# Loading the values of later batches with a casting DMA in GpSimd's queue, in one file with q, k and the expert weights

## Chip, cores and metric

The kernel runs on one NeuronCore of a Trainium2 chip. The metric is device time in microseconds (us), the median of several executions. Smaller is better.

## Reference

Sparse attention in four batches is followed by a mixture of experts that sends a whole batch (a "sentence") to one expert. Cut to what matters:

```python
# q, k, v: (4, 8, 768, 64) fp32
k_sum = k.reshape(B, H, 24, 32, D).max(axis=3)      # one key per block of 32
v_sum = v.reshape(B, H, 24, 32, D).mean(axis=3)     # one value per block
scores_l = q @ k.T / 8, kept where |i - j| < 16     # window
scores_s = q @ k_sum.T / 8 + log(32)                # all 24 blocks
x = softmax([scores_l, scores_s]) @ [v, v_sum]      # (4, 768, 512) over the heads
# experts: w1 (8, 512, 1024), w2 (8, 1024, 512) fp32
logits = x.mean(axis=1) @ w_gate                    # one row per batch
e = argmax(logits); gate = softmax(logits)[e]
out = gate * (relu(x @ w1[e]) @ w2[e])
```

The weights of a batch can be fetched only when its own attention is complete, since the gate chooses the expert.

## The kernel before

**Attention.** A batch has 8 heads in 4 pairs and 768 queries in 12 groups (j) of 64. One group needs 96 window keys and 24 block keys, 120 rows. For a pair, TensorE transposes k (L406) and q (L431), VectorE copies k out of PSUM with the windows laid side by side (L425; ScalarE does that for batch 0, L423) and q (L439), and takes the block maxima (L445). Per pair and half (6 groups) TensorE makes scores (L463), ScalarE the exponential (L474), VectorE multiplies by the mask (L478), TensorE multiplies by the values (L496, called AV here) and VectorE normalizes (L509, L510). Each pair is then transposed (L520) and copied to `xT_b` (L528).

**Values.** The operand of AV is `vblk`, 128 partitions x 12 groups x 8 heads x 65 in bf16, two buffers by the parity of the batch. Rows 16 to 79 of a group are its own 64 values, rows 0 to 15 and 80 to 95 the neighbours' (the halo), rows 96 to 119 the 24 block sums, and column 64 is one, for the softmax's denominator. For batches 1 to 3, SyncE's queue loads v in fp32 into the single buffer `v_f`, one DMA per head (L211). VectorE casts two heads at a time into `vblk` (L295), SyncE copies the halo inside `vblk` (L300, L301), TensorE sums the blocks with the matrix `bind` (L355), VectorE casts the sums to `vsb` (L367), and two DMAs spread them to all 12 groups (L374). Batch 0 loads its halo from HBM.

**Experts.** After the gate (L633 to L694) GpSimd reads the chosen expert's number (L653) and issues the loads of w1 (L664) and w2 (L670), cast to bf16 by the DMA. TensorE makes the hidden layer (L725, 16 half tiles a batch, ScalarE's relu at L740) and the output (L759, 6 tiles, called o; ScalarE scales them at L769 and SyncE stores them, L772). q and k come through GpSimd's queue too, cast by the DMA (L204).

**Order.** The program adds operations with durations and dependencies to a list scheduler, `Sched`. At build time it gives each engine a fixed order. Every engine then runs its own list in order: an instruction that waits holds up all that stand behind it on its engine. `after` fixes only the order of two issues. The file of GpSimd's DMAs is: the chosen w1 and w2 of batch b, the second half of q and k of b+1, the first half of b+2. The loads of v for b+2 stand in SyncE's queue, behind the issue of w2 of b.

Of the kernel before, what the change touches and what calls it, by code (L numbers as in the profile page):

```python
# [12 lines left out]
BF16 = mybir.dt.bfloat16  # L13
# [8 lines left out]
class Sched:  # L22


    SEM = 0.06
    URGENT = 3.0

    def __init__(self):
        self.ops = []
# [37 lines left out]
    def run(self, t0):  # L67
        free = dict(t0)
        rings = {}
        left, users = {}, {}  # L70
        for op in self.ops:
            need = {d["n"] for d in op["deps"] + op["after"]}
            left[op["n"]] = len(need)
            for n in need:
                users.setdefault(n, []).append(op)
        tail = {}
        for op in reversed(self.order(users)):
            tail[op["n"]] = op["dur"] + op["lat"] + (op["dma"] and op["dma"] + 2.0) + max(
                [tail[u["n"]] for u in users.get(op["n"], [])], default=0.0
            )  # L80
# [12 lines left out]
        for op in self.ops:  # L93
            if not left[op["n"]]:
                push(op)
        for _ in self.ops:
            best = None
            for eng, rs in ready.items():
                if not rs:
                    continue  # L100
                t0e = max(free.get(eng, 0.0), min(r for r, _ in rs))
                pick = None
                for r, op in sorted(rs, key=lambda x: x[1]["key"]):
                    start = max(t0e, r)
# [12 lines left out]
            free[eng] = t + op["dur"]  # L117
            op["issued"] = t + op["dur"]
            op["end"] = op["issued"] + op["lat"]
            if op["dma"]:  # L120
                begin = max(rings.get(eng, 0.0), op["issued"] + 0.8)
                other = max([f for e, f in rings.items() if e != eng], default=0.0)
                shared = min(op["dma"], max(0.0, other - begin))
                rings[eng] = begin + op["dma"] + shared
                op["end"] = rings[eng] + 1.2
# [9 lines left out]
def kernel(  # L135
# [10 lines left out]
    nc = tc.nc  # L146
# [5 lines left out]
    QB = 64  # L152
# [55 lines left out]

    def load_v(b, h):
        if b > 0:  # L210
            nc.sync.dma_start(v_f[16:80, :, h, :], v[b, h].rearrange("(j p) d -> p j d", p=QB))  # L211
            return
        j0 = 1 if h == 0 else 0
        nc.sync.dma_start(  # L214
            v_f[:, j0:NJ, h, :],
            bass.AP(
                tensor=v.tensor,
                offset=v.offset + (h * S + j0 * QB - 16) * D,
                ap=[[D, 80], [QB * D, NJ - j0], [1, D]],
            ),  # L220
        )
        if h == 0:
            nc.sync.dma_start(v_f[16:80, 0, 0, :], v[0, 0, 0:QB, :])
# [41 lines left out]
    def setup_dve():  # L265
        for i in range(2):
            nc.vector.memset(vblks[i][64:KW, NJ - 1, :, :], 0.0)
            nc.vector.memset(vblks[i][0:KW, :, :, D : D + 1], 1.0)
        for t in kts:
# [56 lines left out]
    def v_ops(b, loads):  # L326
# [4 lines left out]
        groups = [(0,), (1,)] if b == 0 else [(0, 1)]  # L331
        casts = []
        for c in range(NP):
            on_act = False
            eng = nc.scalar if on_act else nc.vector
            casts.append(
# [5 lines left out]
                )  # L342
            )
        for gs in groups:
            cs = [c for g in gs for c in casts[2 * g : 2 * g + 2]]
# [5 lines left out]
            def vs(b=b, gs=gs, st=st):  # L351
                ps = ops_pool.tile([128, 512], FP32, name="ops")
                for j in range(NJ):
                    for i, hg in enumerate(gs):
                        nc.tensor.matmul(  # L355
                            ps[32 * i : 32 * i + 32, 0 : HW * (D + 1)],
                            lhsT=bind[:, j, :],
                            rhs=vblks[b % 2][0:80, j, hg * HW : (hg + 1) * HW, :],
                            start=(j == 0),
                            stop=(j == NJ - 1),  # L360
                        )
                st["ps"] = ps

            def ev(b=b, gs=gs, st=st):
                n = 32 * len(gs)
                st["sb"] = sm_pool.tile([64, HW, D + 1], BF16, name="vsb")
                nc.vector.tensor_copy(  # L367
                    st["sb"][0:n],
                    st["ps"][0:n, 0 : HW * (D + 1)].rearrange("p (h c) -> p h c", c=D + 1),
                )  # L370

            def bc(b=b, gs=gs, st=st):
                for i, hg in enumerate(gs):
                    nc.sync.dma_start(  # L374
                        vblks[b % 2][KW:NR, :, hg * HW : (hg + 1) * HW, :],
                        st["sb"][32 * i : 32 * i + NB].unsqueeze(1).to_broadcast([NB, NJ, HW, D + 1]),
                    )
# [3 lines left out]
            o_ev = add("DVE", 0.42, [o_vs], ev)  # L381
            sl["first"], sl["readers"] = o_vs, [o_ev]
            o_bc = add("SP", 0.6 * len(gs), [o_ev], bc, dma=0.8 * len(gs))
            for g in gs:
                done.append([hl, o_bc])
        v_ready[b] = done
# [235 lines left out]

        return sequence, xsl, x_ops

    def gate(b, x_ops, w_deps):

        sb = state[b]
        sl, deps = sch.slot("ops", 1)
# [66 lines left out]

        o_lg = add("PE", 0.25, x_ops + deps, lgf, lat=0.2)
        o_mx = add("DVE", 0.7, [o_lg], mxf)
        o_ld = add("POOL", 1.5, [o_mx] + w_deps, ldf)
# [90 lines left out]
        return [o_st(st) for st in range(NST)]  # L789

    casts, bcs = v_ops(0, v_loads)
    moe_last = {}
    w_order = []
    for b in range(B):
        sch.prio = 40.0 if b == 0 else 0.0
        sequence, xsl, x_ops = attention(b)
        nxt = b + 1
        sch.prio = 0.0
        if nxt < B:
            prev = last_T.get(nxt - 2, [])  # L800
            qk_loads[nxt, 0] = qk_loads[nxt, 1] = add(
                "POOL", 1.3, prev, lambda n=nxt: load_qk(n, 0, 4), dma=4.7, after=order_pool
            )
            vl = []
            for h in range(H):
                vl.append(
                    add("SP", 0.6, casts, lambda n=nxt, h=h: load_v(n, h), dma=0.87, after=vl[-1:] + bcs + w_order)
                )

        sch.prio = 40.0 if b == 0 else 0.0  # L810
        sequence()
        w = gate(b, x_ops, moe_last.get(b - 2, []))
        w_order = [w[2]]
        sch.prio = 0.0
        if nxt < B:
            casts, bcs = v_ops(nxt, vl)
            qk_loads[nxt, 2] = qk_loads[nxt, 3] = add(
                "POOL", 1.3, prev, lambda n=nxt: load_qk(n, 4, 8), dma=4.7,
                after=[w[2], qk_loads[nxt, 0]],
            )  # L820
            order_pool = [qk_loads[nxt, 2]]
        moe_last[b] = moe(b, w, xsl)

    sch.run({"PE": 0.0})
# [30 lines left out]
```

## Time and profile before

| What | us |
|---|---|
| Three executions | 228.34, 229.96, 229.79 |
| Median | 229.79 |
| Profiled execution | 229.69 |
| Its span, first to last instruction | 228.1 |
| TensorE busy | 163.5 (72%) |
| VectorE, ScalarE busy | 100.9, 96.9 |
| Mean granted TensorE clock | 0.892 |

The page divides the span into 40 slices of 5.7 us and gives busy shares in tenths. A row of the waits gives who waited for whom, the total in us, how often, and the longest wait. A row of the timeline gives start, duration, engine, line, operation and operands, and in brackets the idle time just before it and what ended that. The row of a DMA queue gives packets, MB and the time its packets took as a share of 16 DMA engines' time in the window.

### The profile page before, as it was taken

Reading aid. Unit: us, or ns where it says so; the run is one execution under the profiler, and the core shown is the slowest. Engines: PE = TensorE matmul, PEld = TensorE weight load, DVE = VectorE, ACT = ScalarE, POOL = GpSimd, SP = SyncE. Lnnn points to the kernel's source line nnn. Section 1 sums busy time; section 2 is a strip of 40 time slices with the busy share of each in tenths; the row PEclk is TensorE's granted clock in tenths of the full one; section 3 lists DMA queues with packets and bytes.
Section 4 is the critical chain, followed back from the end, with each engine's and each line's share of the span. In section 5 each row is a group of like instructions: output and inputs, shape, how many; then the busy total and the mean of one; then the engine's idle time right before and its main releaser. Section 6 shows DMA issues by size and latency. Waiting matters only on the chain.

```text
span 228.1 us, 4604 instructions
## 1 busy us (share of the span) xinstructions
PE 163.5 (72%) x1938; PEld 97.3 (43%) x1960; DVE 100.9 (44%) x207; ACT 96.9 (42%) x182; POOL 24.6 (11%) x43
## 2 busy tenths in 40 slices
PE   0266797478770598993890588994998999089992
PEld 0244675354440465551450455542455544045540
DVE  5364788961302978740302969501269611000000
ACT  2121675334431265553140266623467954025532
POOL 7226000340000000240000000220000002000000
PEclk9999999999995559998598579999799999659998
DMA  6999994299999604399999703199970016990033
GB/s 105 206 183 166 213 174 84 32 165 171 207 197 192 80 3 73 89 156 222 200 196 179 204 0 67 50 166 237 252 139 3 3 50 151 251 194 3 0 152 124
DMA packets 46870, 30.45 MB, mean 133 GB/s; under 512 B 28225, under 2 KB 42145, under 8 KB 46753
## 3 DMA queue, kind: packets, MB, share of 16 engines
q0 software_dynamic: 13264, 14.68, 40.3%
q1 hardware_dynamic: 33584, 15.47, 32.2%
q8 instruction: 15, 0.25, 0.5%
q14 instruction: 7, 0.05, 0.1%
HBM read 36.06 MB, written 6.29 MB: 186 GB/s over the span
## 4 chain that ended last, share of the span: by engine, by line
PE 36%; DMA 28%; SPq 15%; DVE 10%; ACT 5%; issue 3%; POOL 1%; POOLq 1%; ACTq 0%; DVEq 0%
DMA v_f<-in_v_dram 15%; PE hps L725 11%; DMA q_nat<-in_q_dram 9%; SPq L211 9%; PE hps L759 8%; DMA w_sb<-in_moe_w_dram 5%; SPq L214 4%; PE ops L355 3%; PE tps L520 3%; PE tps L431 3%; DVE kT L425 3%; PE kps L406 3%; DVE vblk L295 2%; PE sc L463 2%; PE ops L496 2%
## 5 line engine op out<-in xcount | busy, mean ns | idle before, releaser
L725 PE MATMUL hps<-xT_b,w_sb 128*128 128x256 bf16 (+1 forms) x242 | 55.2, 371 | 14.3 <-DMA w_sb<-in_moe_w_dram 12.6
L740 ACT ACTIVATE hT_sb<-hps 128x512 bf16<-128x512 f32 (+1 forms) x64 | 29.8, 489 | 38.2 <-PE hps L725 36.8
L759 PE MATMUL hps<-w_sb,hT_sb 128*128 128x512 bf16 x184 | 43.2, 380 | 0.6 <-issue 0.3
L725 PEld LDWEIGHTS <-w_sb 128*128 128x128 bf16 x256 | 24.7, 108 | 30.3 <-DMA w_sb<-in_moe_w_dram 12.5
L474 ACT ACTIVATE aT<-sc 128x768 bf16<-128x768 f32 x32 | 25.9, 809 | 14.9 <-PE sc L463 14.6
L406 PE MATMUL kps<-identb,k_nat 96*64 96x96 bf16 x256 | 11.3, 249 | 25.5 <-DVE kT L425 18.0
L478 DVE TENSOR_TENSOR aT<-aT,mask 120x768 bf16<-120x768 bf16 x32 | 17.7, 556 | 23.0 <-ACT aT L474 22.9
L295 DVE CAST vblk<-v_f 80x1536 bf16<-80x1536 f32 x16 | 15.2, 956 | 26.4 <-DMA v_f<-in_v_dram 26.4
L759 PEld LDWEIGHTS <-hT_sb 128*128 128x128 bf16 x192 | 17.8, 98 | 19.8 <-issue 0.2
L769 ACT ACTIVATE o_sb<-hps,gcol 128x512 f32<-128x512 f32 x24 | 16.5, 686 | 22.4 <-PE hps L759 15.4
L528 ACT ACTIVATE xT_b<-tps 128x768 bf16<-128x768 bf16 x16 | 13.0, 810 | 27.4 <-PE tps L520 27.4
L406 PEld LDWEIGHTS <-k_nat 96*64 96x64 bf16 x256 | 9.4, 139 | 28.0 <-issue 20.6
L664 POOL DMA_DIRECT2D w_sb<-in_moe_w_dram x5 | 3.8, 757 | 156.9 <-DVE grec L684 116.8
L496 PE MATMUL ops<-vblk,aT 120*64 120x65 bf16 x384 | 14.4, 220 | 7.2 <-DMA vblk<-vsb 4.1
L510 DVE TENSOR_TENSOR xs<-ops,rv 128x384 bf16<-128x384 f32 x32 | 17.8, 557 | 1.1
L496 PEld LDWEIGHTS <-aT 120*64 120x64 bf16 x384 | 10.8, 130 | 16.4 <-DVE xs L510 4.7
L425 DVE COPY kT<-kps 128x1152 bf16<-128x1152 bf16 x12 | 16.1, 1346 | 0.5 <-PE kps L406 0.5
L463 PE MATMUL sc<-qT,kT 64*128 64x64 bf16 x384 | 13.8, 215 | 3.0 <-ACT aT L474 1.6
L445 DVE TENSOR_REDUCE kmx<-kT 128x24 bf16<-128x768 bf16 x16 | 15.1, 942 | 0.1
L355 PE MATMUL ops<-vblk,bind 80*32 80x260 bf16 x96 | 11.3, 348 | 5.1 <-DVE vblk L295 5.1
L463 PEld LDWEIGHTS <-kT 64*128 64x128 bf16 x384 | 9.7, 109 | 10.6 <-issue 7.1
L509 DVE RECIPROCAL rv<-ops 128x6 f32<-128x6 f32 x32 | 6.1, 191 | 15.7 <-PE ops L496 15.6
(53 smaller groups left out, 110.6 us busy)
## 6 DMA issues: line engine op xcount, KB each, us to landing
w_sb<-in_moe_w_dram POOLq DMA_DIRECT2D x7, 1024.0 KB, 14.8
out_dram<-o_sb SPq DMA_DIRECT2D x24, 256.0 KB, 2.0
v_f<-in_v_dram SPq DMA_DIRECT2D x24, 192.0 KB, 8.5
k_nat<-in_k_dram POOLq DMA_DIRECT2D x6, 384.0 KB, 19.4
q_nat<-in_q_dram POOLq DMA_DIRECT2D x6, 384.0 KB, 20.9
v_f<-in_v_dram SPq DMA_DIRECT2D x7, 240.0 KB, 6.7
vblk<-vsb SPq DMA_DIRECT2D x8, 146.2 KB
vblk<-vblk SPq DMA_DIRECT2D x6, 178.8 KB, 3.8
```

The costliest lines, as they stand in the source:

```text
L211: nc.sync.dma_start(v_f[16:80, :, h, :], v[b, h].rearrange("(j p) d -> p j d", p=QB))
L295: eng.tensor_copy(dst, v_f[:, :, hs, :])
L355: nc.tensor.matmul(ps[32 * i : 32 * i + 32, 0 : HW * (D + 1)], lhsT=bind[:, j, :], rhs=vblks[b % 2][0:80, j, hg * HW : (hg + 1) * HW, :], ...
L406: nc.tensor.transpose(kps[hh * D : (hh + 1) * D, g, 2 : 2 + SP], qk_nat[b][1][:, 2 * pr + hh, g, :], identb[0:SP, 0:SP],)
L425: nc.vector.tensor_copy(kdst, win)
L463: nc.tensor.matmul(sc[:, hh, jj * QB : (jj + 1) * QB], lhsT=sb["kT"][pr][rs, j, :], rhs=sb["qT"][pr][rs, j, :], start=True, stop=True, til ...
L474: nc.scalar.activation(aT, sb["sc"][:, :, 0 : NH * QB], ACT.Exp, scale=SCALE)
L496: nc.tensor.matmul(ops[(j % 2) * QB : (j % 2 + 1) * QB, hh, jj // 2, :], lhsT=aT[0:NR, hh, jj * QB : (jj + 1) * QB], rhs=vb[0:NR, j, 2 * p ...
L510: nc.vector.tensor_tensor(out=sb["xs"][pr][:, hf * NS : (hf + 1) * NS, :, :].rearrange("p s h d -> p h s d"), in0=ops[:, :, :, 0:D], in1=r ...
L725: nc.tensor.matmul(sb["hps"][:, 0 : c1 - c0], lhsT=sb["w1"][:, dt, ft * 128 : (ft + 1) * 128], rhs=sb["xT"][:, dt, c0:c1], start=(dt == 0) ...
L740: nc.scalar.activation(sb["hT"][:, ft, c0:c1], ps["t"][:, 0 : c1 - c0], ACT.Relu)
L759: nc.tensor.matmul(ps["t"], lhsT=sb["hT"][:, ft, st * 128 : (st + 1) * 128], rhs=sb["w2"][:, ft, :], start=(ft == 0), stop=(ft == NFT - 1),)
```

## The change

For batches 1 to 3, v is loaded by GpSimd's queue straight into `vblk` in bf16. The VectorE casts of these batches (four a batch) and their use of `v_f` are gone. All loads of batch b+2 are issued together after w2 of b: first half of q and k, v, second half of q and k. The loads of batch 1 are issued before the first gate. The block sums of both head groups are made by 12 matmuls of 512 columns instead of 24 of 260 (for later batches), land in 24 rows of one of two fixed `vsb` tiles whose ones column is set once, and are spread by one DMA whose packets have 8 x 65 x 2 = 1040 bytes instead of two with 520. Constants of the scheduler's model of shared DMA change too.

```diff
+    SHARE = {"POOL": 0.3, "SP": 2.0}
...
-                shared = min(op["dma"], max(0.0, other - begin))
+                shared = min(self.SHARE[eng] * op["dma"], max(0.0, other - begin))
...
+    vsbs = [const_pool.tile([NB, H, D + 1], BF16, name=f"vsb{i}") for i in range(2)]
...
     def load_v(b, h):
         if b > 0:
-            nc.sync.dma_start(v_f[16:80, :, h, :], v[b, h].rearrange("(j p) d -> p j d", p=QB))
+            nc.gpsimd.dma_start(vblks[b % 2][16:80, :, h, 0:D], v[b, h].rearrange("(j p) d -> p j d", p=QB))
             return
...
         for c in range(NP):
+            if b > 0:
+                casts += loads[2 * c : 2 * c + 2]
+                continue
...
-                    for i, hg in enumerate(gs):
-                        nc.tensor.matmul(
-                            ps[32 * i : 32 * i + 32, 0 : HW * (D + 1)],
-                            lhsT=bind[:, j, :],
-                            rhs=vblks[b % 2][0:80, j, hg * HW : (hg + 1) * HW, :],
...
+                    nc.tensor.matmul(
+                        ps[0:32, 0 : n * D],
+                        lhsT=bind[:, j, :],
+                        rhs=vblks[b % 2][0:80, j, hs, 0:D],
...
+                nc.sync.dma_start(
+                    vblks[b % 2][KW:NR, :, hs, :],
+                    vsbs[b % 2][:, hs, :].unsqueeze(1).to_broadcast([NB, NJ, n, D + 1]),
+                )
...
+    def load_next(n, prev, casts, order):
+        sch.prio = 0.0
+        qk_loads[n, 0] = qk_loads[n, 1] = add(
+            "POOL", 1.3, prev, lambda: load_qk(n, 0, 4), dma=4.8, after=order
+        )
+        vl = []
+        for h in range(H):
+            vl.append(
+                add(
+                    "POOL", 0.9, last_av.get(n - 2, []), lambda h=h: load_v(n, h), dma=1.5,
+                    after=vl[-1:] or [qk_loads[n, 0]],
+                )
+            )
+        qk_loads[n, 2] = qk_loads[n, 3] = add(
+            "POOL", 1.3, prev, lambda: load_qk(n, 4, 8), dma=4.8, after=vl[-1:]
+        )
+        order_pool[:] = [qk_loads[n, 2]]
+        return vl
...
+        if b == 0:
+            vl = load_next(nxt, prev, casts, order_pool)
+        w = gate(b, x_ops, moe_last.get(b - 2, []), order_pool)
...
+        if nxt + 1 < B:
+            vl = load_next(nxt + 1, last_T[b], casts, [w[2]])
```

On GpSimd, before, these rows stand between w2 of batch 0 and the gate of batch 1 (`k_nat_276` belongs to batch 1, `k_nat_802` to batch 2, and `TENSOR_LOAD` reads the expert of batch 1):

```order
L670 DMA w2_sb_730<-in_moe_w2_dram 128x8x512
L204 DMA k_nat_276<-in_k_dram 96x4x512
L204 DMA q_nat_275<-in_q_dram 96x4x512
L204 DMA k_nat_802<-in_k_dram 96x4x512
L204 DMA q_nat_801<-in_q_dram 96x4x512
L653 TENSOR_LOAD ix8_1392
```

Now, at the same place, with batch 2 as `k_nat_822` and the values of batch 2 as `vblk0_103`:

```order
L675 DMA w2_sb_754<-in_moe_w2_dram 128x8x512
L206 DMA k_nat_822<-in_k_dram 96x4x512
L206 DMA q_nat_821<-in_q_dram 96x4x512
L213 DMA vblk0_103<-in_v_dram 64x12x64 x8
L206 DMA k_nat_822<-in_k_dram 96x4x512
L206 DMA q_nat_821<-in_q_dram 96x4x512
L658 TENSOR_LOAD ix8_1314
```

The loads of batch 1 moved ahead of the first gate; all of batch 2, v included, stands ahead of the second gate's weights.

On VectorE, before, the casts of batch 2's values (`vblk0_103`) stand in the middle of batch 1's attention, ahead of the copy of batch 1's third pair of keys (`kT0_105`):

```order
L509 RECIPROCAL rv_997<-ops_978 128x6
L510 TENSOR_TENSOR xs_996<-ops_978,rv_997 128x2x3x64
L295 CAST vblk0_103<-v_f_102 80x12x2x64
L509 RECIPROCAL rv_1020<-ops_1001 128x6
L510 TENSOR_TENSOR xs_996<-ops_1001,rv_1020 128x2x3x64
L295 CAST vblk0_103<-v_f_102 80x12x2x64
L425 COPY kT0_105<-kps_108 128x12x96
```

Now batch 1's third and fourth pair (`kT0_107`, `kT1_108`) are copied ahead of its first normalization, and the cast that is left there is of the block sums:

```order
L430 COPY kT0_107<-kps_110 128x12x96
L483 TENSOR_TENSOR aT_874<-aT_874,mask_115 120x768
L450 TENSOR_REDUCE kmx_892<-kT0_107 128x24
L373 CAST vsb1_106<-ops_876 24x8x64
L444 COPY qT_931<-tps_896 128x768
L430 COPY kT1_108<-kps_110 128x12x96
L450 TENSOR_REDUCE kmx_960<-kT1_108 128x24
L483 TENSOR_TENSOR aT_956<-aT_956,mask_115 120x768
L514 RECIPROCAL rv_1039<-ops_1019 128x6
```

No VectorE instruction in this stretch reads a value of batch 2 any more.

On SyncE, before, the spread of batch 1's block sums (`vsb`) and the eight loads of batch 2's values stand ahead of batch 2's halo:

```order
L374 DMA vblk1_104<-vsb_849 24x12x260 x2
L211 DMA v_f_102<-in_v_dram 64x12x64 x8
L300 DMA vblk0_103<-vblk0_103 16x5720
L301 DMA vblk0_103<-vblk0_103 16x5720
L772 DMA out_0_dram<-o_sb_1322 128x512
```

Now:

```order
L379 DMA vblk1_104<-vsb1_106 24x12x520
L305 DMA vblk0_103<-vblk0_103 16x5720
L306 DMA vblk0_103<-vblk0_103 16x5720
L777 DMA out_0_dram<-o_sb_1359 128x512
```

The halo of batch 2, which waits for all eight loads of its values, now stands directly behind the spread, and the outputs of batch 0 stand behind the halo.

More of the change, by code (lines that the diff above doesn't have):

```diff
@@ L268, in setup_dve @@
             nc.vector.memset(vblks[i][0:KW, :, :, D : D + 1], 1.0)
+        nc.vector.memset(vblks[1][0:16, 0, :, 0:D], 0.0)
+        for t in vsbs:
+            nc.vector.memset(t[:, :, D : D + 1], float(BLK))
         for t in kts:
@@ L344, in v_ops @@
         for gs in groups:
-            cs = [c for g in gs for c in casts[2 * g : 2 * g + 2]]
+            cs = [c for g in gs for c in casts[2 * g : 2 * g + 2]] if b == 0 else casts
             hs = slice(HW * gs[0], HW * gs[-1] + HW)
@@ L379, in v_ops, with bc @@
+            def bc(b=b, n=n, hs=hs, st=st):
+                nc.sync.dma_start(
+                    vblks[b % 2][KW:NR, :, hs, :],
+                    vsbs[b % 2][:, hs, :].unsqueeze(1).to_broadcast([NB, NJ, n, D + 1]),
+                )
             w = cs if b == 0 else cs + [hl]
             o_vs = add("PE", 1.3 * len(gs), w + deps + [bind_setup], vs, lat=0.2)
-            o_ev = add("DVE", 0.42, [o_vs], ev)
+            o_ev = add("DVE", 0.06 + 0.27 * len(gs), [o_vs, dve_setup] + prev, ev)
@@ L382, in v_ops @@
             sl["first"], sl["readers"] = o_vs, [o_ev]
-            o_bc = add("SP", 0.6 * len(gs), [o_ev], bc, dma=0.8 * len(gs))
+            o_bc = add("SP", 0.5, [o_ev], bc, dma=1.0 * len(gs))
             for g in gs:
@@ L623, in attention, with gate @@
         return sequence, xsl, x_ops
-    def gate(b, x_ops, w_deps):
+    def gate(b, x_ops, w_deps, order):
         sb = state[b]
@@ L697, in gate @@
         o_mx = add("DVE", 0.7, [o_lg], mxf)
-        o_ld = add("POOL", 1.5, [o_mx] + w_deps, ldf)
+        o_ld = add("POOL", 1.5, [o_mx] + w_deps, ldf, after=order)
         if b == 0:
@@ L797 @@
         nxt = b + 1
[L798 to L808, printed above, removed]
         sch.prio = 40.0 if b == 0 else 0.0
         sequence()
-        w = gate(b, x_ops, moe_last.get(b - 2, []))
-        w_order = [w[2]]
+        prev = last_T.get(nxt - 2, [])
+        if b == 0:
+            vl = load_next(nxt, prev, casts, order_pool)
+        w = gate(b, x_ops, moe_last.get(b - 2, []), order_pool)
         sch.prio = 0.0
```

31 lines of the change are left out of this document (9 added, 22 removed).

## Prediction

> **What bounds the kernel now.** I read the slices of the page first, then the waits of TensorE and VectorE, then the timeline at the holes, then busy times by stage.
>
> ```profile
> PE   0266797478770598993890588994998999089992
> PEclk9999999999995559998598579999799999659998
> DMA  6999994299999604399999703199970016990033
> ```
>
> TensorE has three holes (slices of 5.7 us): around 70, 122 and 197 us. In the first two the DMA engines are full, and after them the granted clock is low.
>
> ```profile
> PE kps L406 <- DVE kT L425: 18.0, 4, 8.6
> DVE vblk L295 <- DMA v_f<-in_v_dram: 26.4, 8, 8.7
> PE hps L725 <- DMA w_sb<-in_moe_w_dram: 12.6, 3, 6.9
> PE ops L496 <- DMA vblk<-vsb: 4.1, 1, 4.1
> ```
>
> TensorE's largest wait is for the copy of keys L425. The second row shows why that copy is late: VectorE stands at a cast of v. The timeline of both engines at the holes:
>
> ```profile
> 71.81 0.96 DVE L295 CAST vblk<-v_f 80x1536 bf16<-80x1536 f32 x1 [8.72 <-DMA v_f<-in_v_dram]
> 74.31 0.96 DVE L295 CAST vblk<-v_f 80x1536 bf16<-80x1536 f32 x1 [0.85 <-DMA v_f<-in_v_dram]
> 75.19 1.35 DVE L425 COPY kT<-kps 128x1152 bf16<-128x1152 bf16 x1
> 76.59 0.85 PE L406 MATMUL kps<-identb,k_nat 96*64 96x96 bf16 x16 [8.12 <-DVE kT L425]
> 128.00 0.85 PE L406 MATMUL kps<-identb,k_nat 96*64 96x96 bf16 x16 [8.60 <-DVE kT L425]
> ```
>
> So the present batch stands still for values of the next one, which it doesn't need, only because the cast is ahead of its keys in VectorE's list. Busy time by stage (us, then PE, PEld, DVE, ACT, POOL, clock, DMA share, GB/s):
>
> ```profile
> 41.00:188.00 147.00, 111.38 (x1414) 65.32 (x1435) 74.02 (x144) 65.81 (x129) 12.44 (x17) 0.87 0.72 129
> 68.50:76.60 8.10, 0.01 (x2) 0.01 (x3) 3.91 (x6) 0.60 (x1) 0.00 (x0) 0.56 1.22 181
> 76.60:94.00 17.40, 16.16 (x234) 10.46 (x237) 14.48 (x26) 10.11 (x20) 0.00 (x0) 0.71 0.20 42
> 120.00:128.00 8.00, 0.00 (x0) 0.00 (x0) 3.89 (x6) 0.26 (x1) 0.00 (x0) 0.75 1.00 196
> 160.00:188.00 28.00, 26.94 (x376) 15.20 (x383) 15.37 (x32) 18.56 (x36) 0.00 (x0) 0.94 0.41 88
> 200.30:228.00 27.70, 23.59 (x110) 11.76 (x112) 0.00 (x0) 11.32 (x22) 0.00 (x0) 0.87 0.35 91
> ```
>
> From the first gate (41) to the last (188), TensorE works 111.4 of 147 us. The two holes are 16.1 us of the idle 35.6. Where everything has landed (160:188), TensorE is busy 96%.
>
> **The change, part by part.**
>
> *Casts.* Twelve casts of 0.96 us leave VectorE. It is 74 of 147 us busy between the gates, so that time is worth nothing by itself; what counts is that no VectorE row waits for v. TensorE's 8.1 and 8.6 us go. What is late next is the arrival of data, so I follow GpSimd's file.
>
> *What the file costs.* Rows of the DMA queues in three windows: 31 to 37.5 us, where v's loads run alone; 54 to 71 us, where w2, k, q and v share; 186 to 206 us, where the last w1 and w2 run.
>
> ```profile
> q1 hardware_dynamic: 3934, 0.99, 94.0%
> ...
> q0 software_dynamic: 2504, 2.48, 87.6%
> q1 hardware_dynamic: 2953, 0.89, 31.9%
> ...
> q0 software_dynamic: 1568, 2.10, 64.0%
> ```
>
> A 256-byte packet of v takes 94.0% of 16 x 6.5 us / 3934 = 24.9 ns alone and 31.9% of 16 x 17 us / 2953 = 29.4 ns shared. A packet of k, q or w2 (1024 bytes written) takes 87.6% x 272 / 2504 = 95 ns. w1 and w2 together take 64.0% x 20 = 12.8 us of all engines; q and k of a batch are 1536 packets, 1536 x 95 ns / 16 = 9.1 us.
>
> A cast packet of v (256 bytes read, 128 written) is not in this trace. It lies between 24.9 ns and 95 ns, the latter with eight times the bytes. I take 29.4 ns, the shared 256-byte row, the nearest in size: 8 heads x 768 = 6144 packets, 11.3 us a batch (ends 9.6 and 36.5). A file for one batch is then 12.8 + 9.1 + 11.3 = 33.2 us, and with some 4 us for outputs, halo and sums in SyncE's queue 37.2 us. Before, the shares of 54 to 71 us add to 119%, so two queues overlapped by a fifth; one file may lose that, and I sum without overlap.
>
> The Trainium skill, DMA: Bandwidth & Descriptors, section Specifications, speaks against such packets: below 512 B a DMA engine does a read-modify-write and misses line rate. This trace agrees that they are poor by the byte (256 bytes in 29.4 ns, 1024 in 95), and shows no doubling by the packet. If writing 128 bytes doubled the packet all the same, the sum would be that of the first rival below.
>
> *GpSimd's issues.* Eight v DMAs a batch replace SyncE's.
>
> ```profile
> 17.27 0.63 POOL L204 DMA_DIRECT2D k_nat<-in_k_dram  x1
> 17.90 1.30 POOL L204 DMA_DIRECT2D q_nat<-in_q_dram  x1
> 18.10 0.96 DVE L295 CAST vblk<-v_f 80x1536 bf16<-80x1536 f32 x1 [2.43 <-DMA v_f<-in_v_dram]
> 44.84 0.91 POOL L670 DMA_DIRECT2D w_sb<-in_moe_w_dram  x1
> ```
>
> An issue with 1024 packets took 0.91 us, so eight with 768 take at most 7.3 us a batch, inside 11.3 us of transfer, on an engine that is 12.4 of 147 us busy. An issue beside a cast took 1.30 instead of 0.63 us; those casts go for batches 1 to 3, so I add nothing.
>
> *First cycle, from gate 0 to the start of expert 1's first layer.*
>
> ```profile
> 41.23 0.15 DVE L643 COPY lg<-ops 1x8 f32<-1x8 f32 x1
> 43.35 1.50 POOL L664 DMA_DIRECT2D w_sb<-in_moe_w_dram  x2 [22.81 <-DVE grec L684]
> 46.81 2.79 PE L355 MATMUL ops<-vblk,bind 80*32 80x260 bf16 x24
> 52.35 1.49 PE L725 MATMUL hps<-xT_b,w_sb 128*128 128x512 bf16 x3 [2.32 <-DMA w_sb<-in_moe_w_dram]
> ```
>
> Before, v of batch 1 filled the engines until 37.5 us, and they idled to 43 (the digits 4 and 2). Now v costs 11.3 instead of 9.6 there and the second half of q and k, 4.6, follows: 37.5 + 1.7 + 4.6 = 44. The loads of expert 0, issued at 43.35 as before, lose nothing. They and the rest run serially: 44 + 12.8 (w1, w2) + 4.6 + 11.3 + 4.6 (batch 2) + 3 (SyncE's) = 80; then half of 12.8 for the next w1, and 2 to land: 88.7. Gate 1 is no longer at 93 but near 70 by TensorE's list, so this w1 waits for the file. TensorE: all three cycles hold 111.4 + 5.7 us (three o tiles that stand behind the last gate), 39 each; 41 + 39 + the 4 it idles in 42 to 52 + a halo wait of some 4 = 88. Both agree; I take **90**.
>
> *The other cycles.* From the start of an expert's first layer to the next gate the stage 160:188 is the measure, 28 us, plus 2 for scores and transposes that fell ahead of it: 30. From a gate to the next first layer, with an empty file:
>
> ```profile
> 187.81 0.17 DVE lg L643
> 189.88 10.34 DMA w_sb<-in_moe_w_dram
> 200.26 1.89 PE hps L725 x4
> ```
>
> 200.3 - 187.6 = 12.7 us (four o tiles and the block sums, about 10 us, lie beside it). A cycle is 42.7, more than the file's 37.2, so the file is empty at gates 2 and 3. Gate 2 at 120, first layer 132.7, gate 3 at 162.7, first layer 175.4. The rest is as before: 228.1 - 200.3 = 27.8, so the span ends at 203.2.
>
> *Block sums and halo.* 12 matmuls of 512 columns stream 6144 columns, 24 of 260 stream 6240: the 2.79 us stay. VectorE's copy doubles in length (0.42 to at most 0.84 us, thrice), under TensorE's experts. The spread has half the packets and one issue instead of two; worth 0 to the 4.1 us of the last waits row, and I take 0, since AV now stands later in TensorE's list. SyncE's halo waits for eight landings, and behind it stand four outputs; TensorE waits for the halo at the sums, priced with the 4 above. Batch 0 keeps its path; the extra clears in its setup stand beside loads.
>
> The sum is 203.2. The profiled execution took 229.69, 1.6 over its span, and lies 0.1 from the median shown: **204.8 us**.
>
> **The rivals.**
>
> *Packets (slower).* In GpSimd's file every ns of a v packet is 0.384 us a batch. v of batches 1 and 2 lies ahead of w1 of expert 1 with no slack: 0.77 us per ns above 29.4; batch 3 has 42.7 - 37.2 = 5.5 us of slack, so it adds 0.384 from 43.7 ns on. The gain of 25 us is gone at 56 ns, and a doubled packet, 58.8 ns, gives 204.8 + 22.6 + 5.8 = 233 us; at 65 ns it is 240. For it: nothing here writes 128 bytes and casts. Against: both 256-byte rows.
>
> *Starved SyncE (smaller gain).* A full file delays the halo, the sums and the outputs. Medians from issue to landing, all from 93 to 144 us:
>
> ```profile
> out_dram<-o_sb SPq DMA_DIRECT2D x5, 256.0 KB, 8.5
> vblk<-vblk SPq DMA_DIRECT2D x2, 178.8 KB, 3.9
> ```
>
> Those outputs shared with GpSimd's file, that halo had the engines to itself. At 8.5 the halo is 4.6 later in each of three cycles, and TensorE stands at the block sums: 204.8 + 14 = 219. The Trainium skill, same page, section Issuing engines are not separate DMA queues, says that all queues interleave on the same 16 engines, so moving v between queues frees none of them; the 119% above disagrees in part, and the sum would be this rival's.
>
> *Clock (larger gain).* The stage after the first hole ran at 0.71, the stage without holes at 0.94. With 0.94 throughout, the first cycle falls by some 3 us and the others by 2: 198.
>
> *Not what it says.* If the static list, built on the scheduler's own times, puts another wait where the cast stood (keys of the next pair, the halo), the 16 us come back in another form, with the first cycle's gate near 93 again: 228.
>
> **How the numbers follow.** The forecast (200 to 212) has 0.56, starved SyncE (212 to 224) 0.19, the clock (196 to 200) 0.09, not what it says (227.5 to 232) 0.07, slow packets beyond that 0.09. For 8 in 10 the range is 198 to 223. Within 1% of 229.79, about what a measurement of this kernel can tell from no change, lies 0.07; below 0.84, above 0.09.
>
> **What would show it.** In the profile after: no wait of VectorE for `v_f` after batch 0, and L406's wait for L425 near 1 us; no slice with 0 for TensorE between 41 and 160 us; the gates near 70 to 75, 120 and 163; GpSimd's queue busy without a break from 20 to 118 us; v's packets at 25 to 32 ns. The prediction is wrong if the packets are above 44 ns, if TensorE waits over 5 us at the block sums, or if w1 of experts 1 and 2 lands over 5 us after TensorE wants it.

## The result, and the profile after

The changed kernel takes 206.16 us (median of 205.94, 205.95, 206.36 and 208.55), beside 229.38 us for the kernel before on the same chip: a ratio of 0.902, 95% interval [0.894, 0.909]. Forecast were 204.8 us. (Medians here are over all runs of a kernel; the ratios with intervals leave disturbed runs out.) The profiled execution took 205.95 us with a span of 204.4. First the slices of the page (now of 5.1 us) and the row of GpSimd's queue:

```profile
PE   0361979076899589999999679997999993299992
PEclk9999999755558999999999978999999999679999
DMA  6999999992999999799999994699600149970133
q0 software_dynamic: 32080, 17.04, 117.8%
```

The zeros of TensorE in the middle are gone; one new zero stands at 36 to 41 us, where there was none, and behind it a granted clock of 0.5. The DMA engines are full from 5 to 120 us, with one break from 46 to 51 us, around the issue of the first w1 at 48.7. So the queue wasn't busy without a break from 20 to 118 us, as the prediction had it. The share of 117.8% is a warning: with v's packets in it, "took" counts packets that are in flight together, so it is no price of a packet. The waits of TensorE, and VectorE's for v (from the views of the two engines):

```profile
PE hps L730 <- DMA w_sb<-in_moe_w_dram: 8.7, 2, 7.2
PE ops L501 <- issue: 4.0, 1, 4.0
PE tps L525 <- issue: 2.3, 1, 2.3
PE ops L501 <- DMA vblk<-vsb: 1.6, 1, 1.6
PE kps L411 <- DVE kT L430: 0.7, 1, 0.7
DVE vblk L300 <- DMA v_f<-in_v_dram: 6.5, 4, 2.7
```

The wait for the copy of keys fell from 18.0 to 0.7 us, and VectorE waits for `v_f` in batch 0 alone. New are two waits for "issue", in which TensorE waited for nothing that the trace shows. The milestones from the timeline (copies of the gates' logits, the new stall, the block sums, the last wait for w1):

```profile
41.09 0.50 PE L501 MATMUL ops<-vblk,aT 120*64 120x65 bf16 x11 [3.97 <-issue]
46.57 0.15 DVE L648 COPY lg<-ops 1x8 f32<-1x8 f32 x1
82.14 0.15 DVE L648 COPY lg<-ops 1x8 f32<-1x8 f32 x1 [0.77 <-PE ops L638]
126.32 0.15 DVE L648 COPY lg<-ops 1x8 f32<-1x8 f32 x1 [3.15 <-PE ops L638]
164.74 0.15 DVE L648 COPY lg<-ops 1x8 f32<-1x8 f32 x1 [3.38 <-PE ops L638]
53.46 5.30 PE L363 MATMUL ops<-vblk,bind 80*32 80x512 bf16 x12
89.90 2.80 PE L363 MATMUL ops<-vblk,bind 80*32 80x512 bf16 x12
177.51 0.61 PE L730 MATMUL hps<-xT_b,w_sb 128*128 128x512 bf16 x1 [7.21 <-DMA w_sb<-in_moe_w_dram]
```

Gate 0 comes 5.3 us later than before, and the block sums take about twice their former time; both go against the gain. Busy time by stage (columns as in the prediction):

```profile
46.60:82.40 35.80, 30.01 (x411) 18.75 (x413) 20.99 (x45) 17.94 (x38) 11.03 (x15) 0.78 2.07 137
82.40:97.30 14.90, 14.80 (x96) 6.65 (x96) 1.91 (x8) 4.37 (x10) 6.17 (x9) 1.00 0.95 182
97.30:126.00 28.70, 25.34 (x389) 14.55 (x396) 19.75 (x35) 18.73 (x37) 4.09 (x6) 0.94 2.32 151
126.00:140.00 14.00, 12.35 (x89) 5.45 (x90) 4.45 (x11) 4.16 (x8) 1.64 (x2) 1.00 0.85 182
140.00:164.70 24.70, 24.20 (x384) 14.66 (x390) 15.41 (x31) 18.98 (x38) 0.00 (x0) 1.00 0.30 71
177.50:204.40 26.90, 22.73 (x109) 11.53 (x112) 0.00 (x0) 11.20 (x22) 0.00 (x0) 0.92 0.36 93
```

From gate 0 to gate 3, the first five rows, TensorE now works 106.7 of 118.1 us (90%; before 111.4 of 147).

### The profile page after: what moved, and what is told of

The parts are those of the page before. It is cut to its first block, busy times and chain, and to the rows that moved or that the text cites. A ratio compares the mean times of both kernels' runs of the same rounds, so it can differ in the third digit from the quotient of the medians.

```text
span 204.4 us, 4542 instructions
## 1 busy us (share of the span) xinstructions
PE 158.8 (78%) x1903; PEld 92.5 (45%) x1924; DVE 91.0 (45%) x198; ACT 95.6 (47%) x182; POOL 42.9 (21%) x67
## 3 DMA queue, kind: packets, MB, share of 16 engines
q0 software_dynamic: 32080, 17.04, 117.8%
## 4 chain that ended last, share of the span: by engine, by line
PE 62%; DMA 13%; DVE 7%; issue 5%; SPq 5%; ACT 5%; POOLq 0%; ACTq 0%
PE hps L764 19%; PE hps L730 18%; PE ops L363 7%; DMA w_sb<-in_moe_w_dram 5%; DMA vblk<-vsb 5%; SPq L216 4%; PE ops L501 4%; PE sc L468 4%; PE tps L436 4%; DMA v_f<-in_v_dram 3%; PE kps L411 3%; ACT aT L479 3%; PE tps L525 2%; DVE xs L515 2%; DVE kmx L450 1%
## 5 line engine op out<-in xcount | busy, mean ns | idle before, releaser
L730 PE MATMUL hps<-xT_b,w_sb 128*128 128x256 bf16 (+1 forms) x241 | 48.6, 337 | 10.4 <-DMA w_sb<-in_moe_w_dram 8.7
L764 PE MATMUL hps<-w_sb,hT_sb 128*128 128x512 bf16 x186 | 45.2, 389 | 0.5 <-issue 0.2
L730 PEld LDWEIGHTS <-w_sb 128*128 128x128 bf16 x256 | 22.8, 101 | 24.4 <-DMA w_sb<-in_moe_w_dram 8.9
L213 POOL DMA_DIRECT2D vblk<-in_v_dram x24 | 17.8, 754 | 33.3 <-DMA w_sb<-in_moe_w_dram 10.2
L501 PE MATMUL ops<-vblk,aT 120*64 120x65 bf16 x384 | 13.5, 209 | 8.6 <-issue 4.0
L363 PE MATMUL ops<-vblk,bind 80*32 80x512 bf16 (+1 forms) x60 | 16.4, 445 | 4.4 <-DVE vblk L300 4.4
L501 PEld LDWEIGHTS <-aT 120*64 120x64 bf16 x384 | 10.0, 120 | 15.1 <-issue 8.2
L468 PE MATMUL sc<-qT,kT 64*128 64x64 bf16 x384 | 13.0, 208 | 4.5 <-ACT kT L460 2.6
L411 PEld LDWEIGHTS <-k_nat 96*64 96x64 bf16 x256 | 8.9, 137 | 9.5 <-DMA k_nat<-in_k_dram 6.3
## 6 DMA issues: line engine op xcount, KB each, us to landing
w_sb<-in_moe_w_dram POOLq DMA_DIRECT2D x7, 1024.0 KB, 12.5
```

Of the source, the lines that this page charges most:

```text
L213: nc.gpsimd.dma_start(vblks[b % 2][16:80, :, h, 0:D], v[b, h].rearrange("(j p) d -> p j d", p=QB))
L363: nc.tensor.matmul(ps[0:32, 0 : n * D], lhsT=bind[:, j, :], rhs=vblks[b % 2][0:80, j, hs, 0:D], start=(j == 0), stop=(j == NJ - 1),)
L411: nc.tensor.transpose(kps[hh * D : (hh + 1) * D, g, 2 : 2 + SP], qk_nat[b][1][:, 2 * pr + hh, g, :], identb[0:SP, 0:SP],)
L468: nc.tensor.matmul(sc[:, hh, jj * QB : (jj + 1) * QB], lhsT=sb["kT"][pr][rs, j, :], rhs=sb["qT"][pr][rs, j, :], start=True, stop=True, til ...
L501: nc.tensor.matmul(ops[(j % 2) * QB : (j % 2 + 1) * QB, hh, jj // 2, :], lhsT=aT[0:NR, hh, jj * QB : (jj + 1) * QB], rhs=vb[0:NR, j, 2 * p ...
L730: nc.tensor.matmul(sb["hps"][:, 0 : c1 - c0], lhsT=sb["w1"][:, dt, ft * 128 : (ft + 1) * 128], rhs=sb["xT"][:, dt, c0:c1], start=(dt == 0) ...
```

## The experiments

**Part by part.** First the block sums alone, in the kernel before:

```diff
 # kernel before, plus only:
-  24 x matmul(ps[32*i : 32*i+32, 0:260], bind, vblk[0:80, j, 4 heads, :])
-  2 x dma(spread of 4 heads)          # 520-byte packets
+  12 x matmul(ps[0:32, 0:512], bind, vblk[0:80, j, 8 heads, 0:64])
+  1 x dma(spread of 8 heads)          # 1040-byte packets
```

> The kernel before with only the block sums of the change: 12 matmuls of 512 columns instead of 24 of 260, one spread with 1040-byte packets for a batch instead of two with 520. Theory (this part is worth nothing, since the holes at the key transposes set the time): 228 to 231 us. Rival (TensorE's wait of 4.1 us for the spread goes and nothing takes its place): 224 to 226 us.

Measured: 228.64 us, ratio 0.996 [0.991, 1.001]. This part is worth nothing by itself, as the theory said. Then the rest of the change, with the block sums and spreads of before:

> The changed kernel with the block sums of the kernel before: 24 matmuls of 260 columns in two strips of 32 rows and two spreads with 520-byte packets; v of batches 1 to 3 is cast on its way as in the change. In the changed kernel the 12 matmuls of 512 columns took 5.30 us in the first cycle and 2.80 in the others, against 2.79 and 1.51 before. Theory (v's way carries the whole gain, the block sums none): 203 to 208 us, with sums of 2.8 and 1.5 us. Rival (beside a full file the spread with half the packets is needed): the wait for the spread grows by 2 to 5 us in each cycle, 209 to 216 us.

Measured: 205.16 us, ratio 0.888 [0.881, 0.895]. The whole gain is in what this kernel keeps: v's way, the order of the loads and the scheduler's new constants. The sums of this kernel:

```profile
54.74 2.79 PE L362 MATMUL ops<-vblk,bind 80*32 80x260 bf16 x24
89.60 2.57 PE L362 MATMUL ops<-vblk,bind 80*32 80x260 bf16 x22 [2.37 <-DMA vblk<-vblk]
130.32 1.51 PE L362 MATMUL ops<-vblk,bind 80*32 80x260 bf16 x24
```

In two strips of 32 rows 6240 columns take 1.51 us, where one strip takes 2.80 us for 6144: the two strips run beside each other. So the change's sums cost 1.3 to 2.5 us more a batch, which the prediction held to stay equal.

**Is it the cast, the list, or the queue?** Only the plan, no transfer:

```diff
-  add("SP", 0.6, casts, load_v(n, h), dma=0.87, after=...)
+  add("SP", 0.6, casts, load_v(n, h), dma=2.4, after=...)   # kernel before
```

> The kernel before with nothing changed but the time that the scheduler assumes for a transfer of v (2.4 us instead of 0.87), so that the casts of v stand later in VectorE's list, behind copies of keys that they preceded. Same loads, same queues, same casts. Theory (the hole is a cast at the head of VectorE's list, not the volume of v): TensorE's wait for the copy of keys falls from 18 us below 9 us, 212 to 224 us. Rival (v's arrival itself bounds the kernel, so that the wait only moves to another row): 228 to 231 us.

Measured: 219.69 us, ratio 0.963 [0.955, 0.971]. In VectorE's list the first cast of batch 2 moved from 71.8 to 81.8 us, behind copies of keys (timeline):

```profile
73.12 1.35 DVE L425 COPY kT<-kps 128x1152 bf16<-128x1152 bf16 x1
81.82 0.95 DVE L295 CAST vblk<-v_f 80x1536 bf16<-80x1536 f32 x1
```

and TensorE's waits:

```profile
PE ops L355 <- DMA vblk<-vblk: 11.2, 3, 4.7
PE ops L496 <- DMA vblk<-vsb: 6.0, 3, 2.4
```

The wait for the copy of keys is gone, and about ten of the 23 us with it (8.5 by the ratio), with the same loads, queues and casts. So a cast at the head of the list was a true cause. Of TensorE's time 13 us turned into waits for the halo (three times, at the block sums) and for the spread, which follow the casts. Next, v at the same place in GpSimd's file, without the cast:

```diff
-  nc.gpsimd.dma_start(vblks[b % 2][16:80, :, h, 0:D], v[b, h] ...)   # changed kernel
+  nc.gpsimd.dma_start(v_f[16:80, :, h, :], v[b, h] ...)
+  # and the four casts of a batch on VectorE, as before
```

> The changed kernel with v of batches 1 to 3 at the same place in GpSimd's file, but copied in fp32 (256 bytes read and written by a packet) and cast by VectorE as before; SyncE carries no v. It parts the cast on the way from the move to one file. Theory (what counts is that no VectorE row waits for v): the casts wait for v in VectorE's list again and TensorE behind them, 215 to 228 us. Rival (one file in GpSimd's queue, with SyncE free of v, is what helps): 203 to 209 us.

Measured: 208.1 us, ratio 0.904 [0.894, 0.914]; the changed kernel on the same chip took 206.2 us, 0.896 [0.886, 0.906]. My theory fell. The casts stayed on VectorE and did no harm. GpSimd's queue on the page, the casts that open batches 2 and 3 in the timeline, and the waits of VectorE and TensorE:

```profile
q0 software_dynamic: 14800, 19.40, 57.8%
```

```profile
81.98 0.95 DVE L300 CAST vblk<-v_f 80x1536 bf16<-80x1536 f32 x1
118.93 0.95 DVE L300 CAST vblk<-v_f 80x1536 bf16<-80x1536 f32 x1
```

```profile
DVE vblk L300 <- DMA v_f<-in_v_dram: 7.7, 5, 2.9
PE kps L408 <- DVE kT L427: 1.9, 2, 1.6
```

v of batch 2 lands by 74.7 us here, and its casts stand at 82 us in the list, where v is there; in the kernel before two of its four casts stood in the list ahead of v and waited, the second until 74.3. The reading, argued from these times, is that the plan's time for v now fits the true one, since one file in one order has it. The cast on the way is worth at most some 2 us, less than the intervals can part. Now v in SyncE's queue, in the changed kernel:

```diff
-  add("POOL", 0.9, last_av..., load_v(n, h), dma=1.5, after=...)     # changed kernel
+  add("SP", 0.6, casts, load_v(n, h), dma=0.87, after=...)            # fp32, cast by VectorE
```

> The changed kernel with v of batches 1 to 3 loaded in fp32 by SyncE again and cast by VectorE; the order of the q and k loads and the 1040-byte spread stay. Theory (what the change brings is that no cast of a later batch stands in VectorE's list ahead of the copy of keys): the casts wait for v again, TensorE waits at the key transposes 10 to 18 us in all, 220 to 230 us. Rival (the order of the loads or the spread brought the gain): the waits at the key transposes stay below 3 us, 204 to 209 us.

Measured: 225.68 us, ratio 0.983 [0.974, 0.992]. The time came back, but by another wait than expected: at the key transposes TensorE waited 0.4 us for VectorE's copy, but it stood 19.1 us for the spread, which SyncE issues behind eight loads of v. So the order was mended:

```diff
-  after=vl[-1:] or [qk_loads[n, 0]]
+  after=(vl[-1:] or [qk_loads[n, 0]]) + bcs      # behind the spread of the batch ahead
```

> As the first run with v of batches 1 to 3 by SyncE in fp32 and VectorE's casts, but with v of a later batch issued behind the spread of the batch ahead of it in SyncE's list; in that first run the spread stood behind eight loads of v in SyncE's list and TensorE waited 19.1 us for it. Theory (a cast of v then sits at the head of VectorE's list again): TensorE's wait for the spread falls below 6 us and a wait behind casts of v takes its place, 212 to 226 us. Rival (only SyncE's order was wrong there): 204 to 210 us.

Measured: 212.34 us, ratio 0.922 [0.909, 0.934]. Neither account fits: the casts waited 9.5 us in all (6.5 in the changed kernel, all of it for batch 0), but the longest new wait of TensorE went through an output. From the timeline of SyncE and of TensorE, then ScalarE's wait, and last SyncE in the kernel before:

```profile
88.44 17.05 SPq L213 DMA_DIRECT2D v_f<-in_v_dram  x5
105.60 2.81 SPq L774 DMA_DIRECT2D out_dram<-o_sb  x1
...
113.15 0.51 PE L465 MATMUL sc<-qT,kT 64*128 64x64 bf16 x12 [7.57 <-ACT aT L476]
```

```profile
ACT o_sb L771 <- DMA out_dram<-o_sb: 9.5, 1, 9.5
```

```profile
52.58 21.50 SPq L211 DMA_DIRECT2D v_f<-in_v_dram  x7
```

Five issues of v took SyncE 17 us while GpSimd's file was full (in the changed kernel GpSimd issues one in 0.74 us at the median), and the output behind them held ScalarE's buffer, then its list, then TensorE. In the kernel before seven took 21.5 us. That SyncE is rid of loads whose issues take some 3 us each is thus a second part of the gain, which the prediction didn't name. Beside the 206.2 us of the changed kernel on the same chip, v in GpSimd's file instead of SyncE's queue is worth 6.1 us, its casts included. The other 17.7 us, from 230.0 to 212.3, are there with v still in SyncE's queue. How they divide among the order of the q and k loads, the loads of batch 1 ahead of the first gate and the scheduler's new constants (`SHARE`), no run shows: none varies these by themselves.

**What v's transfer costs in the file.** Landings of v's heads in the trace (us, first and last of a batch):

```
batch   changed kernel           uncast                   half packets (16 transfers a batch)
2       69.67 to 80.24           66.34 to 74.73           77.13 to 95.70
3       110.82 to 121.02         115.17 to 125.98         124.22 to 145.84
```

In the changed kernel a head takes 10.57 / 7 = 1.51 us, then 1.46: with 768 / 16 = 48 packets on each engine 31 ns a packet (assumed were 29.4). Two runs tested the price, one with twice the packets and one with none for two batches:

```diff
+  for c0 in (0, D // 2): dma(... columns c0 : c0 + 32)   # changed kernel: two transfers for a head
```

> The changed kernel with each head of v of batches 1 to 3 in two transfers of 32 columns: twice the packets, each with 128 bytes read and 64 written, the same bytes in all. Theory (v's price goes by the packet, some 30 ns each, and the file has no slack in the first two cycles): 11 to 12 us more a batch in the file, gate 1 near 93, 222 to 237 us. Rival (the price goes by the bytes, or the file is hidden behind TensorE): 205 to 211 us. If many small packets in GpSimd's queue hold up TensorE's instructions, the stalls for nothing that the trace shows grow beyond 4.0 and 2.3 us.

Measured: 229.22 us, ratio 0.990 [0.982, 0.9985]: nearly the whole gain is gone.

```profile
PE kps L415 <- DMA k_nat<-in_k_dram: 11.6, 2, 6.5
PE ops L367 <- DMA vblk<-vblk: 10.2, 2, 6.5
PE ops L367 <- DMA k_nat<-in_k_dram: 5.6, 1, 5.6
```

TensorE now waits for keys and halo (of the 11.6 us 6.5 stand at the kernel's start, as in the changed kernel, where it is 6.3). A half packet took 18.57 / 15 / 48 = 25.8 ns in batch 2 and 30.0 in batch 3, so for these cast transfers the price goes by the packet, not by the bytes. (It doesn't carry over to packets of another kind: an uncast head is recorded as 48 packets of 4096 bytes and took 1.20 to 1.54 us.) Batch 2 costs 16 x 1.24 - 8 x 1.51 = 7.7 us more, batch 3 in the same way 11.4, batch 1 (1.48 us for a half head) 11.5: 30.6 us, of which some 21 reached the end (0.990 against the changed kernel's 0.896 and 0.902, of 229 us). The stalls for nothing shown didn't grow: 2.23 us and none.

```diff
 def load_v(b, h):
+  if b > 1: return        # changed kernel; v of batches 2 and 3 isn't loaded
```

> The changed kernel without the loads of v of batches 2 and 3 (these batches compute with the values of v that lie in the buffers). Theory A (TensorE's list sets the time of the cycles and v's transfer is hidden beside it): gates at the same times within 2 us, 203 to 207 us. Theory B (GpSimd's file sets the cycles together with TensorE; a batch of v is some 12 us in it): gates 1 and 2 come 3 to 6 us earlier each, 192 to 200 us. In both the 2.3 us in which TensorE stood near 116 us for nothing that the trace shows should go if v's packets cause them.

Measured: 202.59 us, ratio 0.883 [0.878, 0.889]. Gates 1 to 3 and the stalls:

```profile
80.86 0.15 DVE L649 COPY lg<-ops 1x8 f32<-1x8 f32 x1 [0.76 <-PE ops L639]
120.87 0.15 DVE L649 COPY lg<-ops 1x8 f32<-1x8 f32 x1 [1.47 <-PE ops L639]
159.41 0.15 DVE L649 COPY lg<-ops 1x8 f32<-1x8 f32 x1 [3.38 <-PE ops L639]
```

```profile
PE ops L502 <- issue: 3.2, 1, 3.2
```

This lies between the two expectations: gate 1 came 1.3 us earlier, gates 2 and 3 some 5.4. Two batches of v, some 23.7 us of file, are worth 3.6 us, and the stall of 2.3 us near 116 us went with them. The file is nearly hidden behind TensorE: less of it earns little, but 30.6 us more cost some 21. It stands at the edge.

**The stall ahead of gate 0.** Batch 1's v alone by SyncE:

```diff
-  if b > 0: nc.gpsimd.dma_start(vblks ...)      # changed kernel
+  if b > 1: nc.gpsimd.dma_start(vblks ...)
+  if b == 1: nc.sync.dma_start(v_f ...)          # and batch 1's four casts
```

> The changed kernel with v of batch 1 alone loaded in fp32 by SyncE and cast by VectorE; v of batches 2 and 3 is still cast on its way. In the changed kernel TensorE stood for 4.0 us at 37 to 41 us for nothing that the trace shows, while a packet of the instruction queue took 1.9 us, gate 0 came at 46.6 instead of 41.2 us, and the granted clock was 0.50 from 41 to 60 us. Theory (the many packets of batch 1's v in GpSimd's queue hold up TensorE's instructions there): the 4.0 us go, gate 0 comes near 41 to 42 us, the clock behind it is near 1.0, 198 to 202 us, unless batch 1's casts bring a wait for v back. Rival (the stall has another cause, such as TensorE's new order): it stays, 205 to 208 us.

Measured: 207.61 us (median of 204.51, 204.97, 210.26 and 211.25); no gain that can be told. The stall at 37 to 41 us is gone, gate 0 came at 42.3 us. TensorE was no faster behind it (its block sums took 5.30 us again; the page's 1.00 there is no measurement, as the part on the clock shows). Of the 4.3 us won there, 3 were left at gate 1 (79.24), 2.4 at gate 2 (123.88) and 0.7 at gate 3 (163.99): v of batch 2 landed from 69.0 to 80.3, as in the changed kernel (69.7 to 80.2), and the file went slower: the first w1 took 8.5 us to land instead of 5.3, beside what SyncE had in flight. The stall near 116 us stayed:

```profile
116.47 0.29 PE L504 MATMUL ops<-vblk,aT 120*64 120x65 bf16 x7 [2.04 <-issue]
```

All profiles together: the stall near 40 us (2.2 to 4.3 us) stands in each of the six that load batch 1's v with the cast, and in none of the eight others (nothing of 1.4 us or more there). In those six a 16 KB packet of the instruction queue took 1.9 to 2.4 us around the stall's start; in the others such packets took 1.0 to 1.7 us between 30 and 45 us. That v's many small packets cause the stall is shown by its going with them, in the run above and in the uncast one; that they do it through the delivery of instructions is argued from this coincidence alone, and later in the kernel it doesn't always hold (the uncast version had 2.24 us at 122, the half packets none there, and the kernel before with the new block sums, which casts no v on its way, 2.9 us at 63).

**Spread and clock.**

```diff
-  dma(spread of 8 heads)                # changed kernel
+  for h0 in (0, 4): dma(spread of 4 heads)
```

> The changed kernel with the spread of a batch in two transfers with 520-byte packets instead of one with 1040; the sums stay at 12 matmuls of 512 columns. Theory (the packet size of the spread is worth nothing): 204 to 208 us. Rival (beside a full file each packet of SyncE's queue waits its turn, so twice the packets land later): the spread that took 9.3 us in the first cycle takes 12 to 18 us, and 209 to 216 us in all.

Measured: 205.39 us (median of 201.75 to 206.69). No cost of the smaller packets can be told; TensorE waited 1.1 us for the spread, 1.6 in the changed kernel. Last, the two edits against the changed kernel's own losses together, and that kernel itself beside it:

> The changed kernel with batch 1's v by SyncE and VectorE's casts, and with the block sums of the kernel before (24 matmuls of 260 columns in two strips): both of the edits that took TensorE time away from the changed kernel, together. Theory (TensorE's list sets the cycles, so 4 us of stall and 1.3 to 2.5 us of each batch's sums come off the end): 198 to 203 us. Rival (what TensorE gains ahead of a gate it idles again behind it, where it waits for w1): 203 to 208 us.

> The changed kernel itself, on the same chip as the other three, so that versions less than 2% apart can be set side by side: 204 to 209 us.

Measured: 203.22 us, ratio 0.884 [0.874, 0.893], against 206.21 us, 0.896 [0.886, 0.906]. By its median the combination is the best complete version measured, 1.4% under the changed kernel on the same chip (three of four runs at 202.9 to 203.5, against three of four at 205.3 to 206.5); the intervals of the two ratios overlap, so that it is faster is likely and not proven. Neither account is refuted by this number: of 4.0 us of stall and 3.8 us of sums (2.78, 2.86 and 1.51 us instead of 5.30, 2.80 and 2.81) 3.0 us reached the end, and TensorE waited elsewhere, once 5.6 us for the halo. The second run also bears on the clock. The window 41 to 60 us, first in the profile shown above, then in the same kernel run again:

```profile
41.00:60.00 19.00, 15.16 (x201) 9.90 (x200) 12.75 (x25) 6.54 (x13) 7.45 (x10) 0.50 0.97 136
```

```profile
41.00:60.00 19.00, 15.24 (x206) 9.94 (x202) 13.16 (x26) 6.54 (x13) 7.44 (x10) 1.00 0.91 139
```

The page gives 0.50 and 1.00, and yet TensorE did the same work in the same time, and the executions took 205.95 and 206.50 us. The 1.00 is no measurement. The clock's records in that trace begin at 62.8 us (at 35.1 in the first profile), and the page counts a stretch without a record as full. The matmuls tell the rate themselves (timeline of the second run, then of the kernel before):

```profile
52.96 5.30 PE L363 MATMUL ops<-vblk,bind 80*32 80x512 bf16 x12
60.13 1.89 PE L730 MATMUL hps<-xT_b,w_sb 128*128 128x512 bf16 x4
68.64 1.04 PE L730 MATMUL hps<-xT_b,w_sb 128*128 128x512 bf16 x4
```

```profile
84.66 0.50 PE L463 MATMUL sc<-qT,kT 64*128 64x64 bf16 x12
86.53 0.35 PE L463 MATMUL sc<-qT,kT 64*128 64x64 bf16 x12
```

Until 62 us four matmuls of 512 columns take nearly twice as long as later. Within a run of such matmuls they start 427 ns apart, then 216. So TensorE ran at half rate up to there in both profiles. Where the clock is recorded it agrees: in the kernel before it is 0.50 until 86.5 us, and there the scores become faster. That kernel worked at half rate behind each of its two holes, for 9.9 us (76.6 to 86.5) and for 6.3 us (128.0 to 134.3). An estimate from these times, half of them, is that some 8 us of TensorE's time hung on the holes beside the 16.1 us of the holes themselves. The changed kernel has no such stretch between 62 and 120 us. TensorE's busy time fell from 163.5 to 158.8 us, although its block sums took 5.1 us more. No run holds the clock fixed, so this part of the gain is read from the traces alone.

## Why the prediction was right, and which of its steps were not

- *Casts.* Right in effect: no row of VectorE waits for v after batch 0, and 17.3 us of waits at the key transposes went. The reason was too narrow. "Twelve casts of 0.96 us leave VectorE" was not what was needed: with the casts kept and v in GpSimd's file the kernel takes 208.1 us. What the runs show in its place is that casts must not stand in the list ahead of v's arrival (about 10 us by the plan alone) and that v out of SyncE's queue, whose issues are slow there, is worth some 6 us more.
- *What the file costs.* 29.4 ns a packet, taken from the nearest row; measured were 31. That it came so near is in part luck: it rests on "took", which counts packets that are in flight together. The Trainium skill, DMA: Bandwidth & Descriptors, section Specifications, has writes below 512 B read, modified and written, and a doubling by that was the first rival; neither 128 nor 64 bytes showed one here (31, and 26 to 30 ns).
- *First cycle.* The failed step. Its loads were to "lose nothing" and expert 1's first layer to start at 90; it started at 97.3. Gate 0 was 5.3 us late, 4.0 of it by the stall; gate 1 came at 82 instead of near 70, since TensorE did 30 us of work in between, the part up to 62 us at half rate; and its w1 didn't wait for the file, which emptied at 85.4, within 1 us of w1's issue at 84.8. So "near 70" was 12 us too early, and the wait for the file that was to follow it was not there.
- *The other cycles.* From the first layer to the gate 29.0 and 24.7 us, against 30 and 30; from the gate to the layer 13.7 and 12.8, against 12.7 (the row that it is taken from, with the gate at 187.81, gives 12.5; the 187.6 of the prediction stands in no row); the tail 26.9, against 27.8. In the third cycle's stage stand 96 matmuls of scores against 84 in the stage taken as the measure, and as many transposes, so the 2 us added had little to cover; and the first layer's matmuls of 512 columns took 380 ns each, against 415 in the measure. Errors of +7.3, -1.0, +1.0, -5.3, +0.1 and -0.9 add to +1.2: span 204.4 for 203.2. That they cancel so nearly is luck. The forecast took TensorE's work from the kernel before, with the half rate behind its holes; without it TensorE needed 9.8 us less for the same work, and the 5.1 us of the sums and the two stalls of 4.0 and 2.3 us, which the forecast hadn't, filled the place.
- *Block sums.* "12 matmuls of 512 columns stream 6144 columns", so "the 2.79 us stay", failed: 5.30, 2.80 and 2.81, against 2.79, 1.51 and 1.51, 5.1 us more of TensorE's time. Counting columns overlooked that two strips run beside each other. At the end it costs some 1 to 3 us (205.2 for 206.2; ratios 0.888 against 0.896 and 0.902).
- *Halo and spread.* The wait of 4 us for the halo didn't show; TensorE waited 1.6 us for the spread, for whose packet size no cost could be told, as taken.
- *Rivals.* Slow packets: no, but its slope was right. Its rule (0.77 us per ns for two batches, 5.5 us of slack in the third) gives +25 us for twice the packets at the measured price; some 21 reached the end. Starved SyncE: from 85 to 140 us, beside the file, outputs did land in 8.0 us at the median, near its 8.5 (5.0 over the whole span); but the halos of batches 1 to 3 took 3.7 to 5.7 us, and TensorE never waited for them at the block sums, so the 14 us did not come. Clock: its mechanism was at work, since the half rate behind the holes went with them; its 198 us did not come, as stalls and sums took as much. Not what it says: no wait of its size took the cast's place; the largest new one is the stall of 4.0 us.

## What to carry to other kernels

Where a static list puts work on transferred data, ask when the data really land: a list built on a wrong arrival time stops an engine for data that it doesn't need yet, and here correcting the assumed time alone brought some two fifths of the gain. Count with a hole what runs slower behind it: here some 8 us beside 16. Moving a load into the file whose order you control may be worth more than the compute it takes off an engine. And before trusting that a transfer is hidden, vary it both ways: here removing 24 us of it earned 3.6, and adding 31 cost 21.

## What the runs showed of the hardware

- Two accumulations of 32 output rows each, in different strips, run at the same time: 6240 columns in 1.51 us, one strip 6144 in 2.80. The Trainium skill, TensorEngine Tiling (Array Packing), section Key Properties, says that such tiles operate independently; the traces agree.
- The first block sums took twice as long in every kernel with 512 columns that shows them unbroken (5.30 us against 2.80). Where the clock is recorded, it tells why: 5.30 us at 0.50 and 2.80 at 1.00 in the changed kernel, and in two strips 2.57 us for 22 at 0.50 against 1.51 for 24 at 1.00. A 1.00 ahead of a trace's first record says nothing: 5.30 us stand there too. The Trainium skill, TensorE: Matmul & The Clock Gate, Part 1, tells of half rate until the array has been busy for some 3.4 us; behind the first hole of the kernel before it took 9.9 us of work with pauses of at most 0.33 us, so here the measurement decides.
- With the cast on its way, v is recorded as packets of 128 bytes (6144 a batch); uncast in the same queue it is 384 of 4096 bytes (14800 packets in the queue instead of 32080, 3 x 5760 fewer). A head took 1.46 to 1.52 us cast and 1.20 to 1.54 us uncast, so the time is alike and the number of packets isn't, and only the many come with the stall near 40 us.
- An issue of v on SyncE took 21.5 / 7 = 3.1 us beside GpSimd's file, 0.57 us on SyncE at the kernel's start, and 0.74 us on GpSimd, so the issue time is not a property of the engine alone.
